# Landmark halves swapped over the ScalarE DMA queue, and the next batch's crossbar transposes as a stream of their own beside the GpSimd sums

## The chip, the cores, the metric

One NeuronCore of a Trainium2 chip runs the whole program. The metric is the device time of one execution in microseconds (us). A ratio is the mean time of one kernel's fast runs over that of the kernel before's fast runs of the same rounds, with a 95% interval, so it is not quite the ratio of the medians that stand beside it. The granted clock is the share of its full speed at which PE was let run. The profiled span is some 2 us shorter than the device time. Engines: PE is TensorE, ACT ScalarE, DVE VectorE, POOL GpSimd, SP SyncE; "ACTq", "SPq" and "POOLq" are their queues where they issue transfers.

## The reference, cut to what matters

Nyström attention (8 batches, 8 heads, 576 positions, head size 64, 32 landmarks), then a gated FFN (512 to 1536 to 512).

```python
q_lm = q.reshape(B, H, m, S // m, D).mean(axis=3)          # landmarks: means of 18 rows
k_lm = k.reshape(B, H, m, S // m, D).mean(axis=3)
A, Bm, C = sm(q, k_lm), sm(q_lm, k_lm), sm(q_lm, k)
Z = Bm.transpose(0, 1, 3, 2) / (norms of Bm)
for _ in range(6):
    Z = 2 * Z - Z @ Bm @ Z
x = A @ Z @ C @ v
y = (sigmoid(x @ w_gate) * (x @ w_val)) @ w_out
```

## The kernel before: the parts that matter

The kernel folds Z C v into the two FFN weights. Per batch there is a chain of small steps: q and k are loaded, transposed on the DMA crossbar (`kT`, `qT`), summed on POOL (`s_`), halves combined on PE (`lm`), then the scores `bs`, `sl`, `sa`, the transpose `ct` of the cluster scores, the values `cv`, six Newton steps (`pn`), `wtp`, and the folded weights `U` and `V` (`up`). Beside it runs the bulk: `gp` and `vp` (the gate and value products, which need `U` and `V` of their batch) and `op` (the output product).

All engines' orders are fixed when the program is built. A small model of the engines reckons when each thing will be ready, and the next piece of work is always one that the model holds ready. Nothing is decided on the chip: if a transfer lands later than reckoned, the engine whose next instruction needs it stands, and everything behind it in that queue stands too.

```python
    def load(self, t, mbytes, issue):                # loads of q, k, v: one line, first in, first out
        ...
        start = max(self.free["pool"], issue, self.loads[n - 10])
        end = max(self.free["dma"], start + 2.5) + mbytes / rate
        self.free["dma"] = end

    def turn(self, src, dst):                        # a crossbar transpose, issued from SP
        start = max(self.free["pe"], self.free["sp"], self.landed.get(src.name, 0.0))
        busy = 0.026 * elements / 2048
        self.free["sp"] = start + busy
        end = max(self.free["sp"], self.free["dma"]) + 4.0
        ...

    # front(b), b >= 3: transpose as soon as the load has landed, then the sums on POOL
            if b >= TURN:
                yield need(landed[-1])
                done = turn(t, ..., n, ...)
            ...
            pool.tensor_add(out=s1, ...)  # 128x768, then a second one of 128x768 and two of 128x256
            pool.tensor_copy(out=hl[:, 0], in_=s4)                     # bf16 high part
            pool.tensor_sub(out=hl[:, 1], in0=s4, in1=hl[:, 0])        # bf16 low part
    # landmarks(b): two 256-column matmuls with a 0/1 matrix add the partition halves on PE
    # scale_y(b), just after the values cv:
            if 2 <= b < B - 2:
                for what in "kqv":
                    load(b + 2, what)
```

The last lines: the loads of batch b+2 go out right after the values of batch b are scaled.

The softmax here doesn't subtract the row's maximum and nothing guards it: scores larger than these inputs give would overflow.

## Time and profile before

| kernel before | value |
|---|---|
| device time, median of 3 | 282.44 us (281.95 to 282.44) |
| profiled span, granted clock | 280.0 us, 0.998 |
| chain of waits | 85% PE, 2% DMA |
| first scores `bs` of batches 3 to 7 | 90.8, 123.8, 157.3, 190.9, 223.9 us |
| first `up` of batches 3 to 7 | 113.6, 147.4, 180.9, 213.0, 243.4 us |
| last matmul starts, end | 275.0, 280.0 us |

The views that bound the kernel are in the prediction. One more is needed for what follows: the timeline where batch 3's q and k are transposed. Columns of a timeline: start, length, engine, operation, out and in; in brackets the idle time before it and what ended it.

```profile
62.08 3.64 SPq L362 DMA_TRANSPOSE kT<-kn  x1
...
65.83 2.91 SPq L362 DMA_TRANSPOSE qT<-qn  x1
...
67.57 1.64 POOL L145 TENSOR_TENSOR s_3k<-kT 128x768 f32<-128x768 bf16 x1 [7.92 <-DMA kT<-kn]
```

The transposes hold SP's queue for 3.6 and 2.9 us. POOL's first sum starts 5.5 us after the issue of `kT`. Little else was on the way: the queue that carries the loads, in the stretch from 61 to 70 us (packets, MB, share of 16 engines):

```profile
q0 software_dynamic: 417, 0.31, 22.2%
```

### The profile page before, as it was taken

Reading aid. Unit: us, or ns where it says so; the run is one execution under the profiler, and the core shown is the slowest. Engines: PE = TensorE matmul, PEld = TensorE weight load, DVE = VectorE, ACT = ScalarE, POOL = GpSimd, SP = SyncE. Lnnn points to the kernel's source line nnn. Section 1 sums busy time; section 2 is a strip of 40 time slices with the busy share of each in tenths; the row PEclk is TensorE's granted clock in tenths of the full one; section 3 lists DMA queues with packets and bytes.
Section 4 is the critical chain, followed back from the end, with each engine's and each line's share of the span. In section 5 each row is a group of like instructions: output and inputs, shape, how many; then the busy total and the mean of one; then the engine's idle time right before and its main releaser. Section 6 shows DMA issues by size and latency. Waiting matters only on the chain.

```text
span 280.0 us, 7862 instructions
## 1 busy us (share of the span) xinstructions
PE 265.8 (95%) x3034; PEld 166.7 (60%) x3070; DVE 208.2 (74%) x574; ACT 155.9 (56%) x394; POOL 96.0 (34%) x112
## 2 busy tenths in 40 slices
PE   7899999999699999999999999999999999999993
PEld 5788678656455566465654655456743756467441
DVE  3278899969988888858867887587966979599210
ACT  3375658857157744766437853287615783278200
POOL 8523223943960059500693009910492000000000
PEclk9999999999999999999999999999999999999999
DMA  6999999999359694797819995299933131210242
GB/s 95 188 205 206 205 205 207 204 210 143 84 94 217 129 132 104 114 218 145 157 52 144 208 160 111 75 183 199 163 90 77 37 67 32 75 41 0 77 112 75
DMA packets 60885, 36.69 MB, mean 131 GB/s; under 512 B 33200, under 2 KB 56240, under 8 KB 60848
## 3 DMA queue, kind: packets, MB, share of 16 engines
q0 software_dynamic: 23600, 18.88, 44.2%
q1 hardware_dynamic: 37248, 17.31, 31.3%
q8 instruction: 24, 0.39, 0.5%
q14 instruction: 13, 0.11, 0.1%
HBM read 37.75 MB, written 9.44 MB: 169 GB/s over the span
## 4 chain that ended last, share of the span: by engine, by line
PE 85%; DVE 6%; DMA 2%; issue 2%; ACT 2%; POOL 0%; DVEq 0%; POOLq 0%
PE op L233 31%; PE gp L233 16%; PE vp L233 15%; DMA qn<-in_q_dram 2%; PE pn L233 2%; PE idle_ps L233 2%; DVE ht L145 1%; PE rb L233 1%; PE cv L233 1%; PE sa L233 1%; PE tp_q L238 1%; PE up_1g L233 1%; PE up_0g L233 1%; PE up_2g L233 1%; ACT cl L145 1%
## 5 line engine op out<-in xcount | busy, mean ns | idle before, releaser
L233 PE MATMUL op<-wo_sb,ht 128*128 128x512 bf16 x396 | 106.5, 379 | 2.9 <-issue 1.7
L145 ACT ACTIVATE th<-gp 128x288 bf16<-128x288 f32 x192 | 77.3, 415 | 43.9 <-PE gp L233 30.6
L145 DVE SCALAR_TENSOR_TENSOR ht<-th,vp 128x288 bf16<-128x288 bf16 x192 | 81.4, 449 | 14.1 <-ACT th L145 9.1
L233 PE MATMUL vp<-an,V 128*128 128x288 bf16 x384 | 78.5, 286 | 0.2 <-DVE sy L145 0.2
L233 PE MATMUL gp<-an,U 128*128 128x288 bf16 x384 | 78.5, 286 | 0.1
L233 PEld LDWEIGHTS <-ht 128*128 128x128 bf16 x432 | 38.1, 98 | 31.4 <-issue 6.1
L233 PEld LDWEIGHTS <-U 128*128 128x128 bf16 x384 | 35.6, 98 | 20.2 <-issue 1.3
L233 PEld LDWEIGHTS <-V 128*128 128x128 bf16 x384 | 37.5, 98 | 10.2 <-issue 0.4
L145 ACT ACTIVATE ob<-op 128x512 f32<-128x512 f32 x27 | 16.2, 601 | 37.9 <-PE op L233 33.8
L145 DVE SCALAR_TENSOR_TENSOR sy<-sy,pn 128x384 bf16<-128x384 bf16 x35 | 19.3, 552 | 8.1 <-PE pn L233 8.0
L145 DVE TENSOR_SCALAR ob<-op 128x512 f32<-128x512 f32 x9 | 6.1, 683 | 14.0 <-PE op L233 14.0
L233 PE MATMUL pn<-sy 128*128 128x192 bf16 (+1 forms) x84 | 13.5, 237 | 2.2 <-DVE sy L145 2.2
L233 PE MATMUL idle_ps<-idle_w 128*128 128x256 bf16 x74 | 13.8, 315 | 1.2 <-DVE idle_w L282 1.2
L145 ACT ACTIVATE aexp<-sa 128x288 bf16<-128x288 f32 x32 | 11.2, 415 | 4.8 <-PE sa L233 4.5
L145 DVE TENSOR_TENSOR an<-aexp,rb 128x384 bf16<-128x384 bf16 (+1 forms) x32 | 12.4, 448 | 1.8 <-PE rb L233 1.8
L233 PEld LDWEIGHTS <-sy 128*128 128x128 bf16 x88 | 7.6, 97 | 10.1 <-DVE sy L145 6.9
L233 PEld LDWEIGHTS <-comb 128*128 128x128 bf16 x168 | 8.3, 99 | 3.5 <-DVE V L145 1.3
L233 PEld LDWEIGHTS <-idle_w 128*128 128x128 bf16 x74 | 7.4, 112 | 3.7 <-DVE idle_w L282 1.2
L233 PEld LDWEIGHTS <-WT 64*32 64x32 bf16 x384 | 3.7, 89 | 9.5 <-issue 7.0
L255 POOL DMA_DIRECT2D kn<-in_k_dram x9 | 7.0, 781 | 5.0 <-PE sq L233 2.5
L145 DVE CAST U<-up_0g 128x512 bf16<-128x512 f32 x9 | 6.1, 689 | 3.4 <-PE up_0g L233 3.2
L145 POOL TENSOR_TENSOR s_5k<-kT 128x768 f32<-128x768 bf16 x1 | 1.6, 1637 | 19.3 <-DMA kT<-kn 19.3
(207 smaller groups left out, 370.0 us busy)
## 6 DMA issues: line engine op xcount, KB each, us to landing
vn<-in_v_dram POOLq DMA_DIRECT2D x8, 576.0 KB, 12.7
kn<-in_k_dram POOLq DMA_DIRECT2D x7, 576.0 KB, 7.0
qn<-in_q_dram POOLq DMA_DIRECT2D x7, 576.0 KB, 10.1
out_dram<-ob SPq DMA_DIRECT2D x54, 64.0 KB, 2.0
out_dram<-ob SPq DMA_DIRECT2D x18, 192.0 KB, 2.3
out_dram<-ob SPq DMA_DIRECT2D x18, 128.0 KB, 2.4
wg_sb<-in_moe_w_gate_dram POOLq DMA_DIRECT2D x3, 512.0 KB, 20.4
wv_sb<-in_moe_w_val_dram POOLq DMA_DIRECT2D x3, 512.0 KB, 20.8
```

The source lines that it names most:

```text
L145: f(**kw)
L233: nc.tensor.matmul(**kw)
L238: nc.tensor.transpose(**kw)
L255: nc.gpsimd.dma_start(out=t[:, hs], in_=src[b, hs].rearrange("h (p c) d -> p h (c d)", p=P6))
```

## The change

The intent: take the landmark matmuls off PE by swapping the partition halves of the sums with four 64 KB SBUF-to-SBUF transfers from ScalarE's queue and adding them on POOL; load k and q of the next batch ahead of this batch's sums and transpose them in a stream of their own, so that landmarks come earlier; hold tiled PE work back (up to 3 us) so that it joins other tiled work; end with the last output tile in two halves.

```diff
+    def swap(self, src, dst):
+        start = max(self.free["pe"], self.free["sp"], self.landed.get(src.name, 0.0))
+        self.free["sp"] = start + 0.15
+        end = max(self.free["sp"], self.free["dma"]) + 2.5
...
+    DEFER = {"bs": 1.0, "sl": 1.0, "sa": 3.0, "cv": 0.5, "up": 0.0}
...
+    def turns():                                   # a stream of its own
+        for b in range(TURN, B):
+            yield made(mid_of, b - 2)
+            for what in ("k", "q"):
+                yield made(nat, (what, b))
+                ...
+                yield need(landed[-1])
+                turned_of[(what, b)] = t, turn(...)
...
+            if b >= SWAP and what == "k" and b < B - 1:      # in front(b), ahead of the sums
+                load(b + 1, "k")
+                load(b + 1, "q")
...
+                for c in range(2):
+                    nc.scalar.dma_start(out=other[what][64 * c:64 * c + 64], in_=s4[64 - 64 * c:128 - 64 * c])
+                model.swap(s4, other[what])
+            yield need(other["q"])
+            pool.tensor_add(out=klm, in0=hls["k"], in1=other["k"])
+            ...                                              # and two for bq
+            if b < B - 1:
+                yield made(mid_of, b - 1)
+                load(b + 1, "v")
...
-            if 2 <= b < B - 2:                               # in scale_y(b)
-                for what in "kqv":
-                    load(b + 2, what)
...                                                          # weave(): waits of DEFER us for untiled moments;
...                                                          # ffn2(): last tile in two column halves;
...                                                          # Model.pe(): 2 ns more per matmul
```

## The prediction

> **What bounds the kernel now.** I read the page first (parts 1, 2 and 4), then the stages, then the places where the TensorE (PE) waits, then the few rows that the change touches.
>
> ```profile
> PE 265.8 (95%) x3034; PEld 166.7 (60%) x3070; DVE 208.2 (74%) x574; ACT 155.9 (56%) x394; POOL 96.0 (34%) x112
> PE 85%; DVE 6%; DMA 2%; issue 2%; ACT 2%; POOL 0%; DVEq 0%; POOLq 0%
> ...
> 62.00:90.80 28.80, 26.10 (x316) 16.23 (x319) 26.20 (x65) 15.83 (x39) 13.78 (x15) 1.00 0.85 138
> 90.80:123.80 33.00, 32.63 (x348) 19.87 (x352) 27.45 (x77) 19.32 (x51) 13.77 (x15) 1.00 0.81 134
> 123.80:157.30 33.50, 32.51 (x343) 19.57 (x348) 25.71 (x71) 20.03 (x52) 13.75 (x15) 1.00 0.77 142
> 157.30:190.80 33.50, 31.91 (x335) 18.89 (x340) 26.06 (x72) 18.17 (x49) 13.80 (x15) 1.00 0.84 142
> 190.80:223.80 33.00, 32.52 (x341) 19.26 (x344) 26.00 (x73) 18.94 (x49) 11.51 (x12) 1.00 0.60 109
> ...
> PE pn L233 <- DVE sy L145: 2.2, 3, 1.4
> PE idle_ps L233 <- DVE idle_w L282: 1.2, 1, 1.2
> PE rtp L238 <- DVE rhl L145: 0.9, 1, 0.9
> ```
>
> The chain of waits is 85% PE, and in each batch's stage PE is busy for all but 0.4 to 1.6 us (first number after the comma against the stage's length), except the stage 62 to 90.8, which loses 2.7. So the span is the PE's own work, and a change is worth what it takes off PE's instruction stream, plus the few waits it removes. The last three rows say that those waits are few and mostly for VectorE (DVE). Adding the start-to-start gaps of the matmuls above their own column time, I get 5.2 us of true PE waits after 62 us: 2.7 in the stage 62 to 90.8 and 2.5 in all the later ones (a gap of one missing 512-column record, about 216 ns, is not a wait). Before 38.8 us PE is paced by the loads and runs filler matmuls; that part the change hardly touches.
>
> ```profile
> 195.81 0.28 PE L233 MATMUL s<-bdT 128*128 128x128 bf16 x2
> 196.02 0.32 PE L233 MATMUL sa<-qT,klm 64*32 64x288 bf16 x8
> 196.27 0.60 PE L233 MATMUL op<-wo_sb,ht 128*128 128x512 bf16 x2
> 196.80 0.32 PE L233 MATMUL sa<-qT,klm 64*32 64x288 bf16 x8
> ...
> 122.17 0.38 PE L233 MATMUL lm_4q<-hl_4q,comb 128*128 128x256 bf16 x2
> 122.39 0.59 PE L233 MATMUL op<-wo_sb,ht 128*128 128x512 bf16 x2
> ```
>
> Read the starts, not the durations. Two `op` matmuls take 0.43 us when another full-array matmul follows; here 0.53 pass before the 64x32 tiles begin: 0.10 to go into tiled mode. The eight tiles need about 0.14 and hold PE for 0.25: 0.11 to leave it. And the pair of `lm` matmuls holds PE for 0.22.
>
> ```profile
> 137.40 1.03 DVE L145 TENSOR_TENSOR csum<-csl 128x2 f32<-128x2 f32 x1
> ...
> 136.78 1.64 POOL L145 TENSOR_TENSOR s_5k<-s_5k,kT 128x768 f32<-128x768 f32 x1
> 138.49 1.50 POOL L145 TENSOR_TENSOR s_5k<-s_5k 128x256 f32<-128x256 f32 x2
> ...
> 275.39 0.60 ACT L145 ACTIVATE ob<-op 128x512 f32<-128x512 f32 x1 [4.58 <-PE op L233]
> 276.01 0.79 SPq L882 DMA_DIRECT2D out_dram<-ob  x2
> ```
>
> A DVE addition of two elements per partition takes 1.03 us and ends with the GpSimd (POOL) addition that began before it, 138.42. Last two rows: the tail, one 0.60 us eviction, then two stores issued one after the other, 4.6 us from the eviction's start to the end of the span.
>
> **What the Trainium skill says.** (1) "TensorEngine Tiling (Array Packing)", Key Properties: changing the tiling mode drains the TensorE. The trace agrees, with 0.10 in and 0.11 out. (2) "SBUF — State Buffer", Who interferes with whom: a DVE instruction with two SBUF inputs contends with a GpSimd instruction that reads SBUF, and the loser blocks for the whole instruction. The trace agrees: `csum` above, and `ysc` (minimum 0.16, median 0.48, maximum 1.40 us). (3) "DMA: Bandwidth & Descriptors", Issuing engines are not separate DMA queues: transfers issued from ScalarE run on the same 16 engines, only the sequencer's issue time is saved. No run here issues from ScalarE yet; a store holds SP for about 0.4 us (two in 0.79). (4) "Perfetto Trace Analysis", DMA Instruction — HWDGE: the issuing sequencer is held until the descriptors are made. So each swap holds ScalarE for about such a time.
>
> **The change part by part.**
>
> 1. Landmark sums of batches 3 to 7 leave PE. Removed: 5 batches x 2 (k, q) x a pair of 256-column matmuls. 10 x 0.22 = **2.2 us of PE, all on the path**. With them go the PSUM bank they waited for and three DVE casts of 0.42 per batch, 5 x 3 x 0.42 = 6.3 us of DVE, which is off the path (DVE 74%).
> 2. On POOL, per batch: two casts (0.40) and two subtractions (0.67) go, 2.1 us; three additions of 256 elements per partition come, by the same rows about 0.7 each, 2.1. POOL is 34% busy: no effect on the end by itself.
> 3. The swap: four 64 KB transfers per batch on ScalarE's queue, 20 in all. Landing about 2 us (a 64 KB store lands in 2.0). Latency from POOL's last sum to the landmarks: 2 to 2.5 + 2.1. Before: `hl_4q` ends at 113.5, `lm_4q` runs at 122.2 and the first scores at 123.8, so 10 us went by, most of it waiting for a bank and a turn on PE. The new way is shorter. ScalarE is held 4 x about 0.35 = 1.4 us per batch, in two bursts of 0.7, which the kernel's own schedule doesn't reckon with. ACT is 56% busy; PE could wait for a bank of `gp`. I put **0.5 us** in all (estimate: 10 bursts, 0.05 each, since the 1 us blocks of DVE left no PE wait for a bank).
> 4. Loads of the next k and q issue ahead of the sums, and transposes run as a stream of their own: `s_4k` waited 19.2 us for its transpose. This brings batch b's landmarks forward by 10 us or more. PE isn't starved (stages above), so by itself worth nothing; but the sums then finish before the next batch's small DVE chain, so the collisions at `csum` and `ysc` should go in the later stages. Of 5.2 us of PE waits I take **2.2** as removed: about 1.5 of the later 2.5, and 0.7 of the 2.7 near 62 to 73, where the third batch's transposes start when its loads land, as before.
> 5. Tiled work is held back up to 3 us to join other tiled work. I count 59 tiled groups before, 7 per steady batch (scores `bs`+`sl` 1 or 2, `sa` 1 or 2, `cv` 1, `up` 3). Joining the two `sa`, or the split `sl`, is one per batch; `cv` or `sa` beside an `up` now and then. 6 to 11 groups fewer on the bound part, say 8, x 0.21 = **1.7 us**. The `up` groups of four banks each can't join, with 8 banks.
> 6. The last tile in two column halves: the last eviction is 128 columns on each of two engines, about 0.28 (the 128x128 `s` evictions took 0.29) in place of 0.60, and the two last stores leave from two queues, saving one issue of about 0.4. **0.6 us**. Its 24 matmuls of 256 columns are the same columns.
> 7. The 2 ns more per matmul are only in the scheduler's reckoning; the order of instructions changes, nothing on the chip.
>
> Sum: 2.2 + 2.2 + 1.7 + 0.6 - 0.5 = 6.2; 282.4 - 6.2 = **276.2 us**.
>
> **The rivals.** (a) ScalarE's queue becomes a wait: it takes instructions in order, so if POOL is late (a block by DVE) a swap's wait stands in front of the `th` activations and PE runs out of banks. For: the scheduler books no ScalarE time for it. Against: it emits the swap only when it reckons the sums done, and POOL's durations (1.64, 0.72) are steady. It would cost 0.5 to 1 us per batch: 279 to 281. (b) The collisions only move: earlier sums now meet `bdT`, `bd` and `rhl` of another batch, and the waits stay at 5. Then 278.5. For: POOL's total is the same. (c) Holding tiled work back delays the chain to `pn` and `up`, and PE runs dry between 62 and 90 us, where the `gp` work is scarce: +1 to +2, so 278. (d) Better than thought: all 5.2 waits vanish and 11 groups join: 273. (e) Nothing at all, because the transfers were hidden anyway: excluded for part 1, as PE is the bound and 2.2 us of its work is gone; 280 is the least I expect.
>
> **Range and chances.** The sure terms are 1 and 6 (2.8); 5 is likely; 4 is the widest (0 to 4.5). Range **273.4 to 279.2 us**. The 2% line is at 276.8, close to my middle: faster by over 2% **0.56**, within 2% **0.42**, slower **0.02**.
>
> **What would show it.** No `lm` of batches 3 to 7 and about 20 transfers from ScalarE (1); ScalarE's issues at 0.3 to 0.4 us and no row of PE waiting for `th` (3, against a); `csum` and `ysc` near 0.15 to 0.25 us (4, against b); about 51 tiled groups, `sa` as sixteen in a row (5); first scores of batch 4 well before 123.8 us (4); from the last eviction to the end 4.0 us (6). Wrong would be: PE's waits after 62 us above 5 us, a stage in which PE idles for landmarks or `U`, or the load-paced start longer than 38.8 us.

## The result, and the profile after

The changed kernel takes **296.74 us** (median of 4, 295.15 to 298.6; the kernel before in the same rounds 282.44), ratio **1.0506** [1.0439, 1.0573]: slower by 5%, where I had predicted 276.2 us and given 2% to a clear loss. Results are correct.

From the page of the changed kernel, the granted clock in 40 slices and the chain of waits:

```profile
PEclk9999999999959999996699999999999999999999
...
PE 68%; DMA 14%; DVE 6%; POOL 3%; ACT 3%; issue 2%; ACTq 2%; SPq 0%; DVEq 0%; POOLq 0%
```

The chain was 85% PE and 2% DMA; it is now 68% PE and 14% DMA, 10% of it the transpose `kT` by the chain's own list, and ScalarE's queue has 2%. PE's clock is halved in parts of three slices; in the page of before every slice is at 9. By stage, with the columns of the prediction's table (window, length, busy of PE, PEld, DVE, ACT and POOL with their counts, granted clock, DMA share, GB/s):

```profile
63.00:93.00 30.00, 26.08 (x288) 15.23 (x286) 18.85 (x57) 13.44 (x34) 10.02 (x9) 0.89 0.94 155
...
123.00:158.00 35.00, 27.26 (x294) 14.79 (x292) 23.40 (x65) 13.70 (x37) 18.34 (x18) 0.85 1.15 179
...
158.00:190.00 32.00, 27.74 (x349) 15.81 (x355) 30.44 (x81) 18.73 (x50) 17.03 (x17) 1.00 0.88 150
```

In the stage from 63 us PE is idle for 3.9 us, in that from 123 us for 7.7, and there the clock is 0.89 and 0.85: about 6.6 and 10.5 us at half speed (twice the missing share times the length). The stage from 158 us is idle for 4.3 us at full clock (the like stage before for 1.6); the one from 190 us, 33.5 of 34.0 us busy, is as full as before. So most of the loss lies in the two stages in which batches 3 and 5 are transposed, and some in the one behind the second. Here is the first, batch 3:

```profile
59.59 0.79 POOL L267 DMA_DIRECT2D kn<-in_k_dram  x1
...
60.38 0.77 POOL L267 DMA_DIRECT2D qn<-in_q_dram  x1
...
61.98 7.36 SPq L374 DMA_TRANSPOSE kT<-kn  x1
...
69.45 5.93 SPq L374 DMA_TRANSPOSE qT<-qn  x1
...
75.57 1.64 POOL L152 TENSOR_TENSOR s_3k<-kT 128x768 f32<-128x768 bf16 x1 [14.42 <-DMA kT<-kn]
...
80.52 1.63 ACTq L478 DMA_DIRECT2D s_3k<-s_3k  x2
...
82.25 0.71 ACT L152 ACTIVATE th<-gp 128x288 bf16<-128x288 f32 x2 [6.37 <-POOL s_3q L152]
...
82.71 0.64 PE L244 MATMUL gp<-an,U 128*128 128x288 bf16 x2 [3.92 <-ACT th L152]
```

Read it downwards. The loads of k and q of batch 4 go out at 59.6 and 60.4, just ahead of the transposes of batch 3. The same two transposes that took 3.6 and 2.9 us of SP now take 7.4 and 5.9, and `kT` lands 13.5 us after its issue instead of 5.4. The loads' queue, from 61 to 70 us, carries four times what it did there before:

```profile
q0 software_dynamic: 1767, 1.33, 101.0%
```

So POOL's sum starts at 75.57 instead of 67.57. ScalarE has the swap of that sum next in its order; it stands until the sum is there, and the `th` activations behind it stand too ("6.37" idle). PE fills its banks with `gp` and `vp`, then stands 3.9 us for a `th`, and is at half clock when it goes on (a `gp` pair takes 0.64 where 0.41 is normal). In batch 5 the transposes are longer still, and a second path leads from them to PE:

```profile
118.40 9.22 SPq L374 DMA_TRANSPOSE kT<-kn  x1
...
118.50 0.77 POOL L267 DMA_DIRECT2D kn<-in_k_dram  x1
...
127.79 6.70 SPq L374 DMA_TRANSPOSE qT<-qn  x1
...
134.60 2.79 SPq L934 DMA_DIRECT2D out_dram<-ob  x4
...
134.65 1.64 POOL L152 TENSOR_TENSOR s_5k<-kT 128x768 f32<-128x768 bf16 x1 [14.62 <-DMA kT<-kn]
...
137.49 1.45 SPq L374 DMA_TRANSPOSE ct<-cl  x1
...
138.94 0.69 DVE L152 TENSOR_SCALAR ob<-op 128x512 f32<-128x512 f32 x1 [6.97 <-DMA out_dram<-ob]
...
139.68 0.64 PE L244 MATMUL gp<-an,U 128*128 128x288 bf16 x2 [6.34 <-DVE ob L152]
```

There `kT` takes 9.2 us and lands after 16.1, and PE stands 6.3 us. What ended that stand is not a `th` but DVE's `ob`, which had waited 7.0 us for a store. SP issues the stores of the output too, in its one order with the transposes. `kT` and `qT`, one right behind the other, hold it from 118.4 to 134.5 us; no store leaves in that time, and the three buffers of `ob` stay full. (ScalarE stands at its swap in the same time, until 139.6 us, so both paths end within a microsecond.) The transpose `ct` of batch 4 stood in that queue as well: its input `cl` was complete at 122.6 us, and it left at 137.5, 15 us later; before, a `ct` never waited more than 2.0 us. The model books 3.7 us of SP for such a transpose (`busy` above), and no time for a store.

The longer story is in the chain. `up` of batches 3, 4 and 5 begins at 128.6, 162.7 and 187.9 (before 113.6, 147.4, 180.9); only batch 7 is clearly ahead (234.6 against 243.4), too late to help. The first scores come late in batch 3 alone (100.3, before 90.8); in batches 4 to 7 they are early, by 3.4, 4.3, 13.2 and 21.6 us. What grew is the way from them to `up`: 28.3, 42.2, 34.9, 34.5 and 32.4 us in batches 3 to 7, before 22.8, 23.6, 23.6, 22.1 and 19.5.

What the result is made of, from the starts of the matmuls: gaps over 40 ns after 38.8 us are 27.1 us in all, before 13.1 (+14.0; a wider measure than the prediction's 5.2, with the mode changes in it, for the comparison only); half-clock matmuls cost 5.1; landmark matmuls gone -2.2; the tail 4.1 for 5.0, -1.0. Together +15.9, against the 15.3 by which the span grew. (There are 45 tiled groups for 59; their saved mode changes lie inside the gaps and are not taken off again.)

### The theories

1. **ScalarE's queue** (rival a of the prediction): the swap blocks the activations behind it. The rest of the change is sound.
2. **The chain**: landmarks to `U` has become too long, and PE runs out of `gp` work.
3. **The frozen order**: the new places of the loads put them beside transposes and swaps; these then land much later than the model reckons, and since the order of every engine is frozen, each late landing is a stand. 1 and 2 are then only the forms in which it shows; stores and `ct` behind long transposes in SP's queue are one more, which I had not listed. No run moves the stores to another queue or gives `ob` more buffers, so its share isn't measured by itself.

If 1 holds, another queue mends nearly all; if 2, no reckoning and no queue does; if 3, keeping the transfers apart (and reckoning them as they are) must bring the time back near the prediction.

### The profile page after: what moved, and what is told of

The parts are those of the page before. It is cut to its first block, busy times and chain, and to the rows that moved or that the text cites. A ratio compares the mean times of both kernels' runs of the same rounds, so it can differ in the third digit from the quotient of the medians.

```text
span 295.3 us, 7926 instructions
## 1 busy us (share of the span) xinstructions
PE 271.4 (92%) x3067; PEld 168.9 (57%) x3067; DVE 205.1 (69%) x565; ACT 152.8 (52%) x390; POOL 96.0 (33%) x107
## 3 DMA queue, kind: packets, MB, share of 16 engines
q10 hardware_dynamic: 1712, 1.41, 1.9%
## 4 chain that ended last, share of the span: by engine, by line
PE 68%; DMA 14%; DVE 6%; POOL 3%; ACT 3%; issue 2%; ACTq 2%; SPq 0%; DVEq 0%; POOLq 0%
PE op L244 24%; PE gp L244 13%; PE vp L244 13%; DMA kT<-kn 10%; PE idle_ps L244 2%; PE pn L244 2%; ACTq L478 2%; DMA kn<-in_k_dram 2%; POOL s_3k L152 2%; POOL s_5k L152 2%; DMA s_6k<-s_6k 1%; PE tp_q L249 1%; PE tp_k L249 1%; DMA out_dram<-ob 1%; PE rb L244 1%
## 5 line engine op out<-in xcount | busy, mean ns | idle before, releaser
L244 PE MATMUL op<-wo_sb,ht 128*128 128x512 bf16 (+1 forms) x444 | 116.2, 378 | 0.7 <-DVE sy L152 0.7
L244 PE MATMUL gp<-an,U 128*128 128x288 bf16 x384 | 80.2, 291 | 11.8 <-DVE ob L152 6.3
L244 PE MATMUL vp<-an,V 128*128 128x288 bf16 x384 | 80.0, 291 | 1.4 <-ACT U L152 1.1
L244 PEld LDWEIGHTS <-ht 128*128 128x128 bf16 x444 | 40.6, 99 | 30.0 <-issue 5.0
L152 ACT ACTIVATE ob<-op 128x512 f32<-128x512 f32 (+1 forms) x26 | 15.2, 585 | 33.8 <-PE op L244 30.0
L152 DVE TENSOR_SCALAR ob<-op 128x512 f32<-128x512 f32 (+2 forms) x12 | 7.6, 634 | 24.3 <-PE op L244 17.2
L152 DVE SCALAR_TENSOR_TENSOR sy<-sy,pn 128x384 bf16<-128x384 bf16 x35 | 19.2, 549 | 6.4 <-PE pn L244 6.2
L244 PEld LDWEIGHTS <-sy 128*128 128x128 bf16 x88 | 8.3, 100 | 6.6 <-DVE sy L152 2.6
L152 ACT CAST U<-up_2g 128x512 bf16<-128x512 f32 x7 | 4.1, 584 | 9.3 <-PE gp L244 8.4
L267 POOL DMA_DIRECT2D vn<-in_v_dram x8 | 6.3, 792 | 6.5 <-PE vp L244 3.4
L152 ACT ACTIVATE cl<-sl 128x288 bf16<-128x288 f32 x20 | 8.0, 410 | 0.8 <-PE sl L244 0.7
## 6 DMA issues: line engine op xcount, KB each, us to landing
kn<-in_k_dram POOLq DMA_DIRECT2D x7, 576.0 KB, 11.5
wg_sb<-in_moe_w_gate_dram POOLq DMA_DIRECT2D x3, 512.0 KB, 19.5
```

Source lines behind the costliest of these rows:

```text
L152: f(**kw)
L244: nc.tensor.matmul(**kw)
L267: nc.gpsimd.dma_start(out=t[:, hs], in_=src[b, hs].rearrange("h (p c) d -> p h (c d)", p=P6))
```

## The experiments

Eighteen kernels ran, all with correct results. The medians are of all runs, the ratios of the fast ones alone: defer_only and apart_swap have two slow runs each and before_loads one (medians of their fast runs: 285.8, 281.5 and 284.4 us). First the table, then each.

| run | what it is | median us | ratio to before [95%] |
|---|---|---|---|
| changed kernel | | 296.74 | 1.0506 [1.0439, 1.0573] |
| pool_swap | swap from GpSimd's queue | 291.40 | 1.0311 [1.0249, 1.0374] |
| lm_pe | no swap, landmarks on PE | 287.82 | 1.0190 [1.0141, 1.0239] |
| late_loads | k, q loads after the sums | 300.86 | 1.0659 [1.0614, 1.0705] |
| reckon_late | all transposes reckoned 10 us later | 297.12 | 1.0530 [1.0479, 1.0582] |
| no_defer | nothing held back | 303.24 | 1.0782 [1.0744, 1.0821] |
| defer_only | before + holding back | 288.06 | 1.0158 [1.0097, 1.0219] |
| swap_only | before + swap | 296.61 | 1.0553 [1.0506, 1.0600] |
| swap_reckoned | the same, swap reckoned 5 us | 290.75 | 1.0304 [1.0233, 1.0375] |
| stream_only | before + early loads and stream | 301.26 | 1.0683 [1.0620, 1.0746] |
| tail_only | before + last tile in halves | 281.76 | 0.9991 [0.9925, 1.0057] |
| mended | loads after the landmarks, new reckoning | 286.98 | 1.0194 [1.0121, 1.0267] |
| mended_nd | the same, nothing held back | 294.74 | 1.0463 [1.0384, 1.0541] |
| mended_ct12 | mended, `ct` reckoned 12 us | 290.68 | 1.0329 [1.0273, 1.0384] |
| after_reckoned | changed kernel, reckoning only | 291.92 | 1.0373 [1.0308, 1.0438] |
| before_loads | loads where before has them | 284.56 | 1.0112 [1.0060, 1.0163] |
| before_loads_nd | the same, nothing held back | 283.96 | 1.0104 [1.0058, 1.0149] |
| apart | and no transpose beside a load | 280.03 | 0.9926 [0.9872, 0.9980] |
| apart_swap | and k, q loads away from the swap | 283.25 | 0.9983 [0.9922, 1.0045] |

### Is it ScalarE's queue?

**pool_swap.** The swap is issued by POOL, right behind its own sums.

```diff
-                    nc.scalar.dma_start(out=other[what]...
+                    nc.gpsimd.dma_start(out=other[what]...
```

> The changed kernel with the four swap transfers of a batch issued from GpSimd's queue in place of ScalarE's; nothing else differs. Theory A (ScalarE's queue, which keeps order, stands at a swap that waits for GpSimd's late sums, and the activations behind it hold TensorE's banks): the waits of TensorE at 78.5 us (4.1), 107 to 115 (1.8), 133 to 141 (7.9) and 171 (1.0) go, and with them most of the about 5 us of half clock after the two long ones: 277 to 280 us, mean clock above 0.99. Theory B (the late transposes starve TensorE of landmarks, whoever issues the swap): stays at 293 to 297. Theory C (holding tiled work back is the cost): stays too.

291.4 us: about 5 us better than the changed kernel. The stand at 78 us is gone, as theory 1 says. The one of batch 5 is not:

```profile
134.52 1.64 POOL L152 TENSOR_TENSOR s_5q<-qT 128x768 f32<-128x768 bf16 x1 [10.82 <-DMA qT<-qn]
...
135.63 0.69 DVE L152 TENSOR_SCALAR ob<-op 128x512 f32<-128x512 f32 x1 [6.82 <-DMA out_dram<-ob]
...
136.37 0.64 PE L244 MATMUL gp<-an,U 128*128 128x288 bf16 x2 [6.20 <-DVE ob L152]
```

POOL's sum still waits for the late transpose, and PE still stands 6.2 us, now for `ob` alone: the stores that SP issued right behind `qT`, at 124.5 to 126.1 us, landed at 134.7 to 135.4, just after `qT` itself (134.5). So ScalarE's queue is part of the cost (ratio 1.0506 to 1.0311, two fifths of the loss), but not the cause.

**lm_pe.** No swap at all: the sums go to bf16 parts and to PE as before; loads, stream and holding back as in the change.

```diff
-            if b >= SWAP:
-                hls[what] = s4
-                continue
...
-    for b in range(LATE, SWAP):
+    for b in range(LATE, B):      # landmarks on PE for all batches
```

> The changed kernel without the swap: the landmark halves are summed on TensorE as before the change, while the early loads, the stream of transposes, the holding back of tiled work and the split last tile stay. Theory A: no stand-still of ScalarE, so 278 to 282 us though the transposes are still late beside the loads and 2.2 us of landmark matmuls are back. Theory B or C: 292 or more.

287.82 us: 9 us better than with the swap, though PE has its 2.2 us of landmark matmuls again. Transposes of batch 3 take 6.8 and 6.1 us here too, and PE stands for the sums directly:

```profile
81.55 0.27 PE L244 MATMUL lm_3k<-hl_3k,comb 128*128 128x256 bf16 x1 [2.91 <-POOL hl_3k L152]
```

With no swap in ScalarE's queue a late transpose still ends as a stand of PE. The swap makes it dearer, by the 9 us; by what way, this run doesn't tell.

### Is it the loads, or what the scheduler reckons?

**late_loads.** k and q of the next batch are loaded after the sums, not ahead of them.

```diff
-            if b >= SWAP and what == "k" and b < B - 1:
-                load(b + 1, "k")
-                load(b + 1, "q")
...
             if b >= SWAP:
                 hls[what] = s4
+                if what == "q" and b < B - 1:
+                    load(b + 1, "k")
+                    load(b + 1, "q")
                 continue
```

> The changed kernel with the loads of the next batch's k and q issued after GpSimd's sums instead of ahead of them; the swap stays on ScalarE's queue. Theory A with its first cause (the loads run on the DMA engines beside the transposes, which land after 13.5 and 16.1 us instead of 5.5, so the sums are late and the swap waits): transposes land in 5 to 7 us again, ScalarE no longer stands still, 278 to 282 us; what stays is about 1.1 us of ScalarE held per swap issue. If ScalarE's queue is the cost whatever the transposes do, or theory C holds: above 290.

300.86 us, a miss: worse by 4 us. The transposes of batch 3 are at 3.7 us again, so that half of the reading was right: it is the loads that lengthen them. But `cv` of batch 3 ran only at 121.5 us (before 104.6) and its `up` at 133.0, and PE had run out of other work:

```profile
132.09 0.49 PE L244 MATMUL wtp<-bd,y 128*128 128x128 bf16 x2 [2.49 <-DVE y L152]
```

In that stretch nearly each matmul is a step of the chain that waits for DVE. It was not a transfer that made `cv` late: `ct` of batch 3 landed at 105.6 us, 3.7 after its issue, and PE did not stand in front of `cv`. The order put it there; `turn` reckons a landing behind all loads on the way, which fits, but no run here changes that alone. The loads also meet other transfers now: a swap of batch 3's q takes up to 6.1 us, `kT` of batch 7 holds SP for 7.7.

**reckon_late.** Only a number: each transpose is reckoned to land 10 us later.

```diff
-        end = max(self.free["sp"], self.free["dma"]) + 4.0
+        end = max(self.free["sp"], self.free["dma"]) + 14.0
```

> The changed kernel with its scheduler told that a transpose lands 10 us later than it reckoned, so that the swap's instructions stand later in ScalarE's order; loads, transposes and queues stay. Theory A: transposes still take 10 to 16 us, but ScalarE doesn't wait for them, 278 to 283 us. Theory B (late landmarks starve TensorE): 290 or more, as they come later still.

297.12 us, no gain. The stand at 78 us is gone, but with the `ct` transpose also 10 us later in the plan `up` of batch 3 came at 138.7 us and PE ran dry. A reckoning that is too late costs as much as one that is too early.

### Each part alone

**defer_only**: the holding back on the kernel before.

```diff
+    DEFER = {"bs": 1.0, "sl": 1.0, "sa": 3.0, "cv": 0.5, "up": 0.0}
... and the parts of need() and weave() that use it, and the 2 ns; nothing else
```

> The kernel before with the holding back of tiled work alone (and the 2 ns in the reckoning). If holding back is worth its saved mode switches (about 8 groups of 0.21 us): 279.5 to 281. Theory D (the chain from landmarks to U is as long as a batch's TensorE work, so the 3 us that the scores of queries are held lengthen it and the gp work runs dry): 283 to 289, with first scores to U (bs to up of batch 3) at 26 us or more instead of 22.8.

288.06 us, ratio 1.0158: alone it costs some 4 us. Its profiled run was slow, so I read from it only the count, 49 tiled groups for 59, and as a hint the way from the first scores to `up` of batch 3: 26.0 us for 22.8, as the second expectation had it. The groups were saved, and time was lost.

**swap_only**: the swap on the kernel before, loads as before.

```diff
+    SWAP = 3
+    def swap(self, src, dst): ...
+            if b >= SWAP: ... four transfers from nc.scalar, three additions on POOL
```

> The kernel before with the swap from ScalarE's queue alone; loads and transposes stay as they were, so transposes run with no loads beside them. If the swap is sound by itself and only late sums make ScalarE stand still: sums are on time, no wait of TensorE over 2 us, 279 to 283 us. If ScalarE's queue is a cost whatever the sums do: 286 or more.

296.61 us. Here the transposes of k and q take 2.9 to 4.4 us and PE has no wait over 2.1 us, so it is not theory 1's stand. But the first scores of batch 3 come at 104.3 us (before 90.8) and `up` at 128.3 (113.6). The reason is in the code: `swap` reckons its landing behind *all* loads on the way (`max(free sp, free dma) + 2.5`), while the trace shows 4.2 us from issue to landing for q of batch 3 (1.9 to 7.5 over all). The plan put the landmarks far too late.

**swap_reckoned**: the same with one line changed.

```diff
-        end = max(self.free["sp"], self.free["dma"]) + 2.5
+        end = start + 5.0
```

> The kernel before with the swap from ScalarE alone, as in swap_only, but a swap is reckoned to land 5 us after its issue instead of 2.5 us after all outstanding loads; nothing else. In swap_only the landmarks of batch 3 were done at 93.5 us and their first use stood in TensorE's order at 104.3. Theory E: bs of batch 3 back to 91 to 96 and the time to 279 to 288 us from 296.6. If the order isn't what made swap_only slow: 294 or more.

290.75 us: 6 us back from one number in the scheduler, on the same instructions. First scores of batch 3 at 95.7, `up` at 121.9. This is the cleanest evidence for the frozen order: the instructions are the same, only their order differs. It is still 3% slower than the kernel before, with transposes of 2.9 to 5.3 us; what makes up that rest, no run tells.

**stream_only**: early loads and the transposes' stream, landmarks on PE.

```diff
+            if b >= SWAP and what == "k" and b < B - 1:
+                load(b + 1, "k"); load(b + 1, "q")
+    def turns(): ...
-                for what in "kqv":
-                    load(b + 2, what)
```

> The kernel before with the early loads and the stream of transposes alone; landmarks on TensorE, nothing held back. If the loads beside the transposes are the first cause, a transpose of batch 3 still takes 6 to 7 us of SP's time instead of 3.6, TensorE stands at its landmark matmuls (3 us near 78) and the time is 284 to 288. If early loads are harmless without the rest: 281 to 282.

301.26 us, the worst of the parts: `kT` of batch 3 takes 7.4 us, and PE stands 6.8 us until 139.5, for ScalarE's `ob`, which waited 9.1 us for a store behind `qT` of batch 5 (8.8 us of SP). This is the part that the prediction called "by itself worth nothing". lm_pe has the same loads and stream, with the holding back and the split tail, and takes 287.82 us. So the parts don't add up: 5.5, 6.8 and 1.6% alone, 5.1% together.

**no_defer**: the changed kernel with nothing held back.

```diff
-        return data, banks, None if tile is None else DEFER[tile]
+        return data, banks, None
```

> The changed kernel with nothing held back. Theory A alone (the swap stands in ScalarE's queue): 294 to 298, as the saved mode switches are lost and nothing else changes. Theory D (holding back lengthens the chain): 286 to 292, with bs to up of batch 3 near 23 us instead of 28.3.

303.24 us: in the changed kernel the holding back *saves* 6.5 us, although alone it costs. My reading, not tested by itself: it shifts the tiled work later, and each of these pieces waits for a transfer that is late.

**tail_only**: the last tile in halves on the kernel before.

```diff
+        parts = 2 if t == B * S // 128 - 1 else 1
+        ... two column halves, two evicting engines, two queues for the stores
```

> The kernel before with the split last tile alone. All theories: 0.6 to 1.0 us less, 280.3 to 281 us, and 4.0 us from the last matmul's start to the end instead of 5.0.

281.76 us, ratio 0.9991 [0.9925, 1.0057]. From the last matmul's start to the end it is 4.3 us, before 5.0. A gain of 0.6 is within the interval and can't be told from none.

### Keeping the transfers apart

**mended.** The loads go out after the landmark additions, v of the same batch, k and q of the next; the swap is reckoned 3 us from its issue, the `ct` transpose 5.

```diff
-                load(b + 1, "k"); load(b + 1, "q")        # ahead of the sums
+            if b > SWAP:                                  # after the landmark additions
+                load(b, "v")
+            if b < B - 1:
+                load(b + 1, "k")
+                load(b + 1, "q")
-        end = max(self.free["sp"], self.free["dma"]) + 2.5          # swap
+        end = start + 3.0
-        end = max(self.free["sp"], self.free["dma"]) + 4.0          # turn
+        end = self.free["sp"] + 5.0 if src.name.startswith("cl") else max(self.free["sp"], self.free["dma"]) + 4.0
```

> The changed kernel, its transfers rearranged: v of this batch and k, q of the next are loaded after the landmark additions, so that neither transposes nor swaps run beside loads, and the scheduler reckons a swap to land 3 us after its issue and the softmax transpose 5 us after, not behind all outstanding loads. Theory E (the order of every engine is frozen at build by reckoned landing times; the change makes transfers meet that were apart, the reckoning is wrong by up to 10 us both ways, and the engines stand at instructions placed too early or get them too late): transposes land in 5 to 7 us, no wait of ScalarE or TensorE over 2 us, U of batch 3 at 114 to 120 instead of 128.6 and 275 to 282 us. If the swap or the holding back is bad in itself: above 288.

286.98 us: 10 us better than the changed kernel. It lies between the two expectations. First scores of batch 3 at 88.1, transposes of k and q of 3.1 to 6.0 us. What PE still stands for, twice (3.4 and 4.2 us, and half clock after each):

```profile
118.35 0.80 POOL L267 DMA_DIRECT2D vn<-in_v_dram  x1
...
119.90 0.77 POOL L267 DMA_DIRECT2D qn<-in_q_dram  x1
...
122.75 1.74 SPq L374 DMA_TRANSPOSE ct<-cl  x1
...
135.27 0.56 PE L244 MATMUL cv<-vn,ct 96*32 96x64 bf16 x48 [3.42 <-DMA ct<-cl]
```

The `ct` transpose is issued behind three loads and lands 12.5 us later (before 3.9). The loads have found the next transfer of the chain.

**mended_nd**: the same, nothing held back.

```diff
-        return data, banks, None if tile is None else DEFER[tile]
+        return data, banks, None
```

> As mended, with nothing held back. Theory E: 275 to 283 us, within 3 us of mended; the difference is what holding back is worth once the transfers keep their reckoned times (7 to 10 groups of 0.21 us saved against about 4 us of longer chain).

294.74 us, with stands of 4.5, 4.8 and 5.7 us at the same `cv`: earlier work waits longer for the same late `ct`.

**mended_ct12**: mended, with the `ct` transpose reckoned as measured there (12 us) and the swap 5.

```diff
-        end = self.free["sp"] + 5.0 if src.name.startswith("cl") else ...
+        end = self.free["sp"] + 12.0 if src.name.startswith("cl") else ...
-        end = start + 3.0
+        end = start + 5.0
```

> The run with the loads after the landmark sums (286.98), with the transpose of the cluster scores reckoned 12 us after its issue (there 5; it took 12.5 beside the loads) and a swap 5 us (there 3). If PE stood there only because its order put the values too early: the stands of 3.6 and 4.3 us at cv and the 3 us of half clock go, 277 to 281. If the time is needed anyway because U comes later by as much: no such stand, but the time within 2 us of 287.

290.68 us, a miss for the first expectation. The stands at `cv` are gone, but PE is out of work around 180 to 189 and 248 to 257 us, where steps of the chains (`pn`, `wtp`, `up`) wait 0.4 to 1.6 us each, mostly for DVE. And 12 us was no longer the right number: `ct` landed after 3.7 to 8.3 us here. Whether the chain is too long as such (theory 2) or the plan is now late isn't told apart.

**after_reckoned**: the changed kernel with the landing times set near the long ones measured, the loads left in its places.

```diff
-        end = max(self.free["sp"], self.free["dma"]) + 2.5          # swap
+        end = start + 5.0
-        end = max(self.free["sp"], self.free["dma"]) + 4.0          # turn
+        end = self.free["sp"] + 8.0 if src.name.startswith("cl") else max(self.free["sp"] + 13.0, self.free["dma"] + 4.0)
```

> The changed kernel with nothing but the scheduler's numbers changed: a swap lands 5 us after its issue (in place of behind all loads), the transposes of k and q 13 us after their issue, that of the cluster scores 8 us. If the order frozen on wrong landing times is the whole cause, 276 to 283. If wrong numbers are only part, and the longer transposes (7 to 9 us of the queue, 13 to 16 us to landing) also lengthen the chain to U beyond what the matmul work on hand can cover: 286 to 293, with no stand of 4 us at the ScalarE activations, but PE short of work ahead of U of batches 3 and 5. If the reckoning has no part: 295 to 298.

291.92 us: the middle expectation in time. Reckoning alone gives back a quarter of the loss (ratio 1.0506 to 1.0373). It still has a stand of 5.9 us until 137.4, again for an `ob`: stores issued behind `qT` from 127.4 us on landed from 135.9, just after it (135.8).

**before_loads** and **before_loads_nd**: everything of the change, but the loads back where the kernel before has them; swap reckoned 5, `ct` 8. The second holds nothing back.

```diff
-                load(b + 1, "k"); load(b + 1, "q")        # ahead of the sums
-                load(b + 1, "v")                          # after the landmarks
+            if 2 <= b < B - 2:                            # in scale_y(b), as before
+                for what in "kqv":
+                    load(b + 2, what)
```

> The changed kernel with the loads of q, k and v put back where the kernel before has them (batch b+2, just after the values of batch b are scaled), and with the waits reckoned as the traces show them (a swap lands 5 us after its issue, the transpose of the cluster scores 8 us after). In the run with the loads after the landmark sums (286.98) what PE still stood for, 3.4 and 4.2 us, was the transpose of the cluster scores, issued behind three loads and landing 12.5 us later. If what costs is loads beside the transposes and swaps that the order hangs on: that transpose lands in under 7 us again, no PE stand of over 3 us, half-clock time under 1 us, and 278 to 283 us. Rival (the tail, the holding back or the swap itself costs, whatever the loads do): 287 or more, as in the run with the holding back alone (288.06) or the swap alone with the longer reckoning (290.75).

> The same with nothing held back (every DEFER wait none). In the changed kernel the holding back was worth 6.5 us (303.24 without it), with the loads after the sums 7.8 (294.74 against 286.98). If that worth came only from giving late transposes a few us more, it should be gone here: within 2 us of the run it is sent with, and some 55 to 59 tiled groups. If it is the saved changes of tiling mode, it should still be about 2 us slower; if 6 or more slower, the holding back does something else that I don't have.

284.56 and 283.96 us, ratios 1.0112 and 1.0104. With the loads back and the landings reckoned, both at once, four fifths of the loss are gone. The expected 278 to 283 was not reached. The profiled run of the first was slow, so I read the second: `ct` lands in 4.0 us again (median), but there are still two stretches of half clock, 3.4 us each. The holding back is worth nothing either way here, as the expectation for late transposes says. What is left shows in its timeline, batch 4:

```profile
122.00 1.64 POOL L152 TENSOR_TENSOR s_5k<-kT 128x768 f32<-128x768 bf16 x1 [7.83 <-DMA kT<-kn]
...
122.20 1.62 DVE L152 TENSOR_SCALAR Bc<-E,rr 128x32 bf16<-128x32 f32 x2
...
124.14 1.43 DVE L152 TENSOR_TENSOR bdT<-blk,Bt 128x128 bf16<-128x128 bf16 x2
...
125.49 0.36 PE L244 MATMUL s<-bdT 128*128 128x128 bf16 x2 [1.41 <-DVE bdT L152]
```

The POOL sums of batch 5 begin 5 us after the first scores of batch 4 and run beside its small DVE chain. `Bc`, two instructions of 0.24 each, takes 1.62; `bdT`, two of 0.22, takes 1.43, and PE waits 1.41 for it. That is the prediction's rival (b), "the collisions only move": `csum` and `ysc` are at 0.16 us in all batches, as predicted, and others pay. Also two transposes still took 7.1 and 7.4 us: k's starts when k has landed, while q and v are on the way.

**apart**: before_loads_nd, and k's transpose waits for v's load as well.

```diff
                 yield need(landed[-1])
+                if b > TURN and what == "k":
+                    yield made(nat, ("v", b))
+                    yield need(nat[("v", b)][1][-1])
```

> The run with the loads put back and nothing held back (283.96), with one more change: the transpose of k waits until the load of v of the same batch has landed too, so that no transpose runs beside a load. There the transposes of batches 4 and 5 still took 7.1 and 7.4 us, beside the loads of q and v, and the GpSimd sums of batches 5 to 7 began just as the small VectorE chain of the batch before started, so that four of its operations ended only with a GpSimd addition and PE stood four times for 1.3 to 1.6 us. The gate also moves those sums by some 5 us, past that chain. The scheduler reckons the same end for both. If transfers beside each other and the moved collisions were what was left of the loss: all transposes under 4.5 us, no PE stand over 1 us between the clusters' matmuls n and s, PE waits after 38.8 us under 10 us, and 276 to 281. If the remaining loss lies in something else that the change brought (the swaps, the tail, the order of the tiled work): 283 to 286, with the same sum of waits spread elsewhere.

**280.03 us** (5 rounds), ratio **0.9926** [0.9872, 0.9980]: the only version whose interval lies below 1. It is 0.7% faster than the kernel before, which is inside the 2% line, and 5.5% better than the changed kernel (0.9926 / 1.0506). All transposes are at 3.1 to 4.3 us, `Bc` and `bdT` never exceed 0.25, the granted clock is 1.0. Two `csum` take 1.3 and 1.4 us again, as one did in the kernel before: the collisions have moved, not gone. PE's waits, in the wide measure, are 16.8 us, not under 10, and more than the 13.1 of the kernel before. So the gain is not in waits removed. The landmark matmuls (-2.2 us) and the tail (-1.0) stand against +3.7 of gaps; by the matmuls' column times some 1.7 us more of PE's work also lies before 38.8 us here, which I did not follow up. Together that is the 1.1 us by which the span is shorter. What remains is this, batch 6:

```profile
174.53 0.79 POOL L267 DMA_DIRECT2D kn<-in_k_dram  x1
...
185.90 0.71 POOL L152 TENSOR_TENSOR bq<-s_6q 64x256 bf16<-64x256 f32 x1 [8.30 <-DMA s_6q<-s_6q]
...
186.67 0.22 PE L244 MATMUL bs<-klm,bq 64*32 64x32 bf16 x8 [1.39 <-POOL bq L152]
```

POOL issues the three loads right behind its sums; the swap of q leaves ScalarE at 177.8, flies beside them and lands after 8.2 us, against 2.4 for the swap of k just before them. PE stands 1.4 us for the landmarks; in batches 3 and 5 it is 0.8 and 0.7 us.

**apart_swap**: the loads of k and q go ahead of the sums, once q is transposed; the next transposes wait for the landmarks.

```diff
+            if b >= SWAP and what == "k":
+                yield made(turned_of, ("q", b))
+                yield need(done, turned_of[("q", b)][1])
+                if b < B - 1:
+                    load(b + 1, "k"); load(b + 1, "q")
+                ...                                       # in turns(): yield made(lm_of, b - 1)
-                for what in "kqv":
-                    load(b + 2, what)
+                load(b + 2, "v")
```

> The run with the gated transposes (280.03), whose trace shows what PE still waits for: in batches 3, 5 and 6 the first scores stood 0.9 to 1.6 us (and 0.5 more) for the landmarks, since the swap of q flew beside the three loads that the GpSimd queue issued right behind the sums, and landed 8.2 us after its issue, against 2.4 for the swap of k ahead of them. Here the loads of k and q of the next batch are issued after the transpose of q and ahead of the sums, and the next transposes wait for the landmarks; only the load of v stays where it was. If the swap beside loads is the last of the loss: the swaps of q land in under 6 us, no stand over 1 us at the first scores, 276 to 279. If the sums, which now wait for both transposes and for two load issues, make the chain to U longer than the matmul work on hand covers: such stands gone, but PE waits elsewhere and 280 to 284.

283.25 us (281.5 for the fast runs), ratio 0.9983 [0.9922, 1.0045]: no better than the kernel before, and not what I hoped. The profiled run was slow, so only what doesn't hang on the clock: the swaps of q land in 2.3 to 6.3 us and no stand at the first scores is left, but transposes of 6.5, 8.5 and 7.1 us are back, and the collision with POOL has moved to the norms of the other scores:

```profile
L152 DVE TENSOR_TENSOR rhl<-ra,rhl x8: 199/201/2453, 23.3 to 228.3; 128x40 bf16<-128x40 f32 x8
```

Columns: operation, minimum, median and maximum in ns. One of eight took 2.45 us, and the longest wait of PE in this profile, 2.4 us, is that of `rtp` for `rhl`. In kind the second expectation held: such stands gone, waits elsewhere.

## Why the prediction was wrong, by its own steps

**What bounds the kernel** was right about the kernel before and was used wrongly. That PE was busy for all but 1 us of a stage was read as slack elsewhere. But the full PE was there because the frozen order fitted the landing times of that arrangement. It said nothing of another one.

**Part 1** (landmark matmuls, 2.2 us): they are gone, as predicted. It was not on its own a gain: lm_pe, which keeps them, is 9 us faster than the change.

**Part 2** (POOL unchanged): right, 96.0 us busy before and after.

**Part 3** (swap, 0.5 us) was too small in three terms. Holding ScalarE: 20 issues take 13.2 us by the trace, 2.6 per batch, not 1.4. The landing: 1.9 to 6.8 us (median 3.0), not 2. And the sentence "The new way is shorter" failed in three batches of five: from POOL's last sum to the first scores it is 14.9, 10.2, 8.6, 14.7 and 15.8 us in batches 3 to 7, before 12.2, 11.5, 11.2, 11.6 and 12.9. Rival (a) was named, with the right mechanism ("if POOL is late ... PE runs out of banks") and was put aside because POOL's durations are steady. They are; what was late was POOL's input, the transpose. It was about 5 us (pool_swap).

**Part 4** is the step that failed: "This brings batch b's landmarks forward by 10 us or more. PE isn't starved (stages above), so by itself worth nothing", with 2.2 us of waits taken as removed. The 19.2 us that it read as `s_4k` waiting for its transpose are POOL's idle time between two batches. I costed the loads and transposes as moved, not as moved beside each other, and left out what else stands in SP's queue. The trace shows a `kT` beside loads at 7.4 and 9.2 us of the queue and 13.5 and 16.1 to landing, against 3.6 and 5.4 without. Batch 3's first scores came 9.5 us later, not 10 earlier; those of batches 6 and 7 did come 13 and 22 earlier, but `up` hung on the transfers after them, such as a `ct` held back 15 us. In place of 2.2 us of waits removed, the gaps in PE's stream grew by 14.0 us and half clock took 5.1. stream_only, which is this part alone, costs 6.8%; putting the loads back and reckoning the landings takes the change from 1.0506 to 1.0112; the reckoning alone, to 1.0373. So theory 3 holds for most of the loss, and it has two sides: the longer transfers themselves, with what stands behind them in SP's queue, and an order made for shorter ones. Shown for the second: swap_only against swap_reckoned, 6 us from one number.

**Part 5** (groups, 1.7 us): the count was right and more (45 for 59), the time wasn't: alone the holding back costs 1.6% (defer_only), beside late transfers it saves (no_defer, mended_nd), with the transfers in order nothing (before_loads against before_loads_nd). I can't show any gain of a saved mode change in the device time.

**Part 6** (tail, 0.6 us): 0.7 us in the trace of tail_only, not resolved in its time.

**Part 7** ("nothing on the chip") is literally true and missed the point: what is only in the scheduler's reckoning decides the order, and the order was worth 6 us in one pair and 4 to 5 in another, by other numbers of the reckoning (no run changed the 2 ns alone).

**Rival (b)** came true: in the changed kernel `csum` and `ysc` stay under 0.6 us, but `bdT` takes up to 1.7 us and `Bc` 1.6, and in before_loads_nd PE waits for them. **Rival (c)**, holding back makes the chain longer, fits defer_only, at some 4 us and not 1 to 2. The rivals were costed one by one at 1 to 5 us; none was "two transfers slow each other".

What stays open: the 3.8 us between apart (280.0) and the prediction (276.2). Its trace shows swaps beside loads and PE waiting for them, but the run that moved those loads gained nothing, so I can't say that this is the rest. Which part of apart's gain comes from the separate transposes and which from the sums moved past the DVE chain isn't told apart either, as one gate did both.

## What to carry to other kernels

Where every engine's order is frozen when the program is built, a move of a transfer is not free because its engine has time: list what is in flight beside it, in both places, and what else waits in the queue that issues it, and take the durations from a trace with the same neighbours. A busy PE says that the present arrangement fits, not that another has slack. When such a change loses, first put the transfers back and correct the reckoned landing times; here this, with nothing held back and no transpose beside a load, turned 5% lost into 0.7% won.

## What the Trainium skill lacked or had wrong

- "DMA: Bandwidth & Descriptors", Rules for kernel authors, says that a transpose next to ordinary DMAs needs nothing. That is about correctness, and results were correct; but nothing there tells of the time. A crossbar transpose of 576 KB beside loads held its queue for 5.9 to 9.2 us and landed after 8.1 to 16.1, against 2.9 to 3.9 and 4.9 to 6.7 apart from them. Stores issued behind such a transpose in the same queue landed only after it: in pool_swap four issued from 124.5 us on landed from 134.7, the transpose at 134.5.
- The same page, Issuing engines are not separate DMA queues, says that transfers from several engines interleave, and that the issue is usually small. No figure for the effect is given: a 64 KB SBUF-to-SBUF swap landed in 1.9 to 3.0 us alone and in up to 8.4 beside three loads, and its issues held ScalarE for 0.47 to 1.5 us each.
- "SBUF — State Buffer", Who interferes with whom, has both kinds of DVE instruction that were held here: two SBUF inputs (`bdT`, 1.30 us for 0.22) and a tensor by a scalar (`Bc`, 1.55 for 0.24). My prediction cited only the first. Nothing was wrong; what it can't say is that several such instructions in one chain each wait in turn, 1.62 and then 1.43 us.
- "TensorE: Matmul & The Clock Gate", HAM oscillation, gives as the abstract rule no idle gaps of PE over about 3.4 us. The two long stands of the changed kernel, 3.9 and 6.3 us, agree: half clock set in 2.3 us into each and lasted 6.8 and 10.2 us (from 135.7 us on it held over a second stand, of 1.1). But keeping single stands under 3.4 us was not enough: before_loads_nd has two stretches of half clock with no stand over 1.4 us, swap_reckoned one of 6.8 us with stands of 1.4 and 2.0. The rule as stated gives no figure for such short stands in a row.
- No page has a warning that an order frozen at build time must be made for the landing times of transfers with their neighbours: the same instructions took 296.6 and 290.8 us with one reckoned landing changed.
